# Last rows of the down weights by GpSimd's queue, and one value part ahead of their products, in a gated attention and feed-forward decode kernel

## The chip, the core and the metric

The kernel runs on one core of a Trainium2 chip. A core has TensorE (PE, with its weight loads shown apart as PEld), VectorE (DVE), ScalarE (ACT), GpSimd (POOL) and SyncE (SP), which run their own instruction streams and meet through semaphores, and 16 DMA engines that move data from device memory into the on-chip tiles of 128 partitions. The metric is the device time of one launch in microseconds (us). Before the change the median of 3 runs is 2518.33 us (2518.11 to 2518.47).

## The reference, cut to what is computed

One token decodes through a mix of two blocks: attention over a cache of 65,536 positions with 32 heads of 128, and a gated feed-forward block of width 1,792.

```python
def _A_ref(x, k_cache, v_cache, wq, wo):
    q = (x @ wq).reshape(B, Sq, H, Dh).transpose(0, 2, 1, 3)
    scores = jnp.einsum("bhqd,bhkd->bhqk", q, k_cache) * (Dh ** -0.5)
    p = _softmax(scores, axis=-1)
    o = jnp.einsum("bhqk,bhkd->bhqd", p, v_cache)
    return o.transpose(0, 2, 1, 3).reshape(B, Sq, H * Dh) @ wo

def _B_ref(x, w_gate, w_up, w_down):
    return (_silu(x @ w_gate) * (x @ w_up)) @ w_down

g = _sigmoid((x * gate_w).sum(-1, keepdims=True))
out = g * _A_ref(...) + (1 - g) * _B_ref(...)
```

All tensors are bfloat16. K and V have 537 MB each; all weights together are about 13.8 MB.

## The kernel before

K and V of a head come in two halves of 8.39 MB, each 256 cache rows per partition in 128 partitions. The big tile `ring` holds both halves of K (from byte 0 and 32 KB), both of V (96 KB and 112 KB), and, before the first and after the last use of those places, the weights: the query weights at first, then the output weights, gate and up weights, and the down weights (`WD`, from byte 64 KB, where the second half of K lay).

SP issues every large load, in one queue, in the order of its program: for each head the next K half, the V half, the other K half, the other V half, each as soon as PE or DVE has read what lay there (semaphores `ktd` for transposed K chunks, `va1` and `vbd` for read V halves). For each K chunk DVE transposes (L314) and PE takes the scores (L401). When a head's scores are complete, DVE takes the maximum, POOL reduces it over the partitions (L216), ACT takes the exponentials (L251) and POOL their sum (L218), and PE multiplies the values.

PE's program consists of named blocks joined by branches. `pe_ka` has a head's first 16 score chunks, `pe_vb` the second half of the previous head's values, `pe_kb` the last 16 score chunks and the first half of this head's values. The values of `pe_vb` come in the six parts of `PARTS`, with a semaphore each from `MARKS`: the first three (rows 192 to 256, 0 to 64, 64 to 128) by `flow`, 16 matmuls a part into `psW` (L417); then DVE copies `psW` to `brow` (L327, for the last head L355), PE adds its rows up (L452), and `values` does the other three parts with one matmul per row (L408). For the first 31 heads one load brings all six parts.

After the last head's scores the branch goes to `pe_mlp`. It does gate and up products (L488), waits for the activations `s_gu` and the down weights `s_wd`, multiplies the first 11 of the 14 down-weight columns (`WD_CUT`, `whole`, L428), lets ACT copy the row to `brow` (L266), puts that row into the two banks of the result (`rows`, L423 and L424), and jumps to `pe_vb` for the last head's second half. `pe_end` then adds the last three down-weight columns, each with its own semaphore (`s_wd1` to `s_wd3`), and the last head's part of the output product; DVE and ACT write the row out.

At the end of SP's list stand therefore: gate weights, up weights, the first 11 columns of the down weights, the last head's second value half in the six parts (the second to sixth after `va1`), and the last three columns of the down weights. All are issued by SP (L145).

Of the kernel before, what the change touches and what calls it, by code (L numbers as in the profile page):

```python
# [5 lines left out]
P = 128  # L6
# [4 lines left out]
V_A, V_B = 96 * KB, 112 * KB  # L11
# [15 lines left out]
def bass_gated_mix__mha_block_cached__swiglu_ffn__decode_kernel(  # L27
# [13 lines left out]
    _, H, S, Dh = A_k_cache.shape  # L41
    D = A_wq.shape[0]
    F = B_w_gate.shape[1]
    Dc = D // P
    FC = F // P
# [7 lines left out]
    PER = 2 * NCH  # L53

    with ExitStack() as ctx:
# [6 lines left out]
        def sem(name):  # L62
# [42 lines left out]
        hx = [kt[:, b, 0:FW].bitcast(F32) for b in range(3)]  # L105
        gu = kt[:, 3, 0:FW // 2].bitcast(BF16)
        guT = kt[:, 3, FW // 2:FW].bitcast(BF16)
        names = ("s_x s_wq s_k0a s_k0b s_ka s_kb s_va s_vb s_wo s_woc s_wg s_wu s_wd s_wd1 s_wd2 s_wd3 s_p2 s_p3 s_p4 s_p5 s_p6 "
                 "s_ones s_qd s_ramp s_rampT s_id s_sel s_z s_zb s_e1 s_g s_xT s_xTb s_q s_qTb s_qs s_zq s_h s_sig s_gu s_dch s_ach "
                 "ktd qkd va1 vbd s_mx s_ar s_nb s_exp s_pb s_L s_li s_otn s_o s_om s_y s_br s_fl s_flc s_id4 s_qr s_qc s_wod s_o31 s_y0 s_y1 s_fin s_out s_hot")  # L110
        sm = {n: sem(n) for n in names.split()}
# [7 lines left out]
        def at(byte, n):  # L119
            return ring[:, byte // 2:byte // 2 + n]  # L120

        WQ, WO, WG, WU, WD = 144 * KB, 0, 0, 14 * KB, 64 * KB
        PARTS = ((192, 256), (0, 64), (64, 128), (128, 168), (168, 184), (184, 192))
        FLOW = 3
        MARKS = ("s_vb", "s_p2", "s_p3", "s_p4", "s_p5", "s_p6")
        WD_CUT = FC - 3
        wq_ap = at(WQ, Dc * H * Dh).rearrange("p (c n) -> p c n", c=Dc)
        wg_ap = at(WG, Dc * F).rearrange("p (c m j) -> p c m j", c=Dc, j=FC)
        wu_ap = at(WU, Dc * F).rearrange("p (c m j) -> p c m j", c=Dc, j=FC)
# [12 lines left out]
        @block.sync  # L142
        def _(sp):
            def load(dst, src, s):
                sp.dma_start(dst, src).then_inc(sm[s], 16)  # L145

            def place(kind, h, u, s):
                byte = {"k": (K_A, K_B), "v": (V_A, V_B)}[kind][u]
                src = kv_dram[kind][:, u]
                if isinstance(h, int):  # L150
                    src = src[h]
                else:
                    src = src[bass.ds(h, 1)].rearrange("h p n -> (h p) n")
                load(at(byte, ROWS * Dh), src, s)

            k0 = kv_dram["k"][0, 0]
            k1 = kv_dram["k"][0, 1]
            half = ROWS * Dh // 2
            load(at(K_A + 2 * half, half), k0[:, half:2 * half], "s_ka")
            load(at(K_A, half), k0[:, 0:half], "s_k0a")  # L160
            load(at(K_B + 2 * half, half), k1[:, half:2 * half], "s_k0b")
            sp.wait_ge(sm["ktd"], NCH // 2)
            load(at(K_B, half), k1[:, 0:half], "s_kb")
            sp.wait_ge(sm["s_q"], 1)
            place("v", 0, 0, "s_va")

            def head(r, late):
                sp.wait_ge(sm["ktd"], r * PER + (PER - NCH // 2))
                place("k", r + 1, 0, "s_ka")
                sp.wait_ge(sm["va1"], r + 1)  # L170
                place("v", r, 1, "s_vb")
                if late:
                    wo_dram = A_wo.rearrange("(p j) n -> p (j n)", j=32)
                    for q in range(2):
                        sp.wait_ge(sm["ktd"], r * PER + (PER + 3 * NCH // 4 + q * NCH // 4))
                        load(at(WO + q * 16 * KB, 16 * D), wo_dram[:, q * 16 * D:(q + 1) * 16 * D], "s_wo")
                sp.wait_ge(sm["ktd"], r * PER + (PER + NCH // 2))
                place("k", r + 1, 1, "s_kb")
                sp.wait_ge(sm["vbd"], r + 2)
                place("v", r + 1, 0, "s_va")  # L180

            with nc.Fori(0, L - 1, engines=[ET.SP]) as i:
                head(i, False)
            head(L - 1, True)
            sp.wait_ge(sm["s_wod"], 1)
            load(at(WG, Dc * F), B_w_gate.rearrange("(p c) f -> p (c f)", c=Dc), "s_wg")
            load(at(WU, Dc * F), B_w_up.rearrange("(p c) f -> p (c f)", c=Dc), "s_wu")
            sp.wait_ge(sm["ktd"], PER * H)
            wd_dram = B_w_down.rearrange("(p c) n -> p (c n)", c=FC)
            load(at(WD, WD_CUT * D), wd_dram[:, 0:WD_CUT * D], "s_wd")  # L190
            last = kv_dram["v"][L, 1]
            for n, ((r0, r1), s) in enumerate(zip(PARTS, MARKS)):
                if n == 1:
                    sp.wait_ge(sm["va1"], H)
                load(at(V_B + r0 * 256, (r1 - r0) * Dh), last[:, r0 * Dh:r1 * Dh], s)
            for j, s in ((FC - 3, "s_wd1"), (FC - 2, "s_wd2"), (FC - 1, "s_wd3")):
                load(at(WD + 2 * j * D, D), wd_dram[:, j * D:(j + 1) * D], s)

        @block.gpsimd
        def _(pool):  # L200
            nc.gpsimd.memset(xTz[:], 0.0).then_inc(sm["s_qd"], 1)
            nc.gpsimd.memset(qd[:], 0.0).then_inc(sm["s_qd"], 1)
            for m, n in enumerate(MARKS[1:]):
                nc.gpsimd.memset(hbuf[:, m], 0.0).then_inc(sm[n], 16 * L)
            nc.gpsimd.memset(hot[:], 0.0).then_inc(sm["s_hot"], 1)
            pool.wait_ge(sm["s_id"], 1)
            pool.wait_ge(sm["s_hot"], 1)
            nc.gpsimd.tensor_copy(hot[:, 31:128:32], ident[:, P - 4:P])
            for je in range(4):
                off = 64 * (je // 2) + je % 2  # L210
                last = nc.gpsimd.tensor_copy(sel[:, je, :].rearrange("p (g d) -> p g d", g=4),
                                             ident[:, off:off + 63:2].unsqueeze(1).to_broadcast([P, 4, 32]))
            last.then_inc(sm["s_sel"], 1)
            for h in range(H):
                pool.wait_ge(sm["s_mx"], h + 1)
                nc.gpsimd.partition_all_reduce(amx, mxs, P, RMAX).then_inc(sm["s_ar"], 1)  # L216
                pool.wait_ge(sm["s_exp"], h + 2)
                nc.gpsimd.partition_all_reduce(Lt, rsum, P, RADD).then_inc(sm["s_L"], 1)  # L218

        @block.scalar  # L220
        def _(act):
# [140 lines left out]
        def _(pe):  # L362
# [14 lines left out]
            for b, bank in enumerate((psY, psZ)):  # L377
                for c in range(Dc):
                    for k in range(4):
                        n0 = (4 * b + k) * D  # L380
# [49 lines left out]
            only = [ET.PE]  # L430
# [14 lines left out]

            with nc.body("pe_vb", valid_engines=only):
                i = nc.snap(head, min_val=1, max_val=H)
                for n, ((r0, r1), s) in enumerate(zip(PARTS, MARKS)):
                    if n == FLOW:
                        pe.wait_ge(sm["s_flc"], i + 1)  # L450
                        for e in range(4):
                            nc.tensor.matmul(psO[:, 0:1], brow[:, e * Dh:(e + 1) * Dh], id4[:, e:e + 1],  # L452
                                             start=e == 0, stop=False)
                    pe.wait_ge(sm[s], i * 16)
                    if n < FLOW:
                        last = flow(V_B, 1, range(r0, r1), False, n == FLOW - 1)
                        if n == FLOW - 1:
                            last.then_inc(sm["s_fl"], 1)
                        continue
                    last = values(V_B, 1, range(r0, r1), False, n == len(PARTS) - 1)  # L460
                last.then_inc(sm["vbd"], 1)
                nc.br_lt(left, 2, on_true="pe_end", on_false="pe_next", engines=only)
# [17 lines left out]
            with nc.body("pe_mlp", valid_engines=only):  # L480
                pe.wait_ge(sm["s_wg"], 16)
                pe.wait_ge(sm["s_wu"], 16)
                pe.wait_ge(sm["s_woc"], 1)
                for w, bank in ((wg_ap, psY), (wu_ap, psZ)):
                    for c in range(Dc):
                        for g in range(4):
                            cols = w[:, c, 32 * g:32 * g + 32, :].rearrange("p m j -> p j m")
                            last = nc.tensor.matmul(bank[32 * g:32 * g + 32, 0:FW], xTz[:, 32 * c:32 * c + 32], cols,  # L488
                                                    start=(c == 0), stop=(c == Dc - 1))
                    last.then_inc(sm["s_h"], 1)  # L490
                pe.wait_ge(sm["s_gu"], 1)
                pe.wait_ge(sm["s_wd"], 16)
                for j in range(WD_CUT):
                    last = whole(guT[:, 32 * j:32 * j + 1], wd_ap[:, j, :], stop=(j == WD_CUT - 1))
                last.then_inc(sm["s_y"], 1)
                pe.wait_ge(sm["s_br"], 1)
                rows(onesr[0:1, 0:1], brow[0:1, :], first=True)
                nc.br("pe_vb", engines=only)

            with nc.body("pe_wo", valid_engines=only):  # L500
                pe.wait_ge(sm["s_otn"], H + 1)
# [62 lines left out]
```

## Time and profile before

| what | us |
|---|---|
| median of 3 runs | 2518.33 |
| the profiled execution, as timed | 2518.01 |
| its span, first to last instruction | 2516.6 |
| DVE busy | 1249.7 |
| PE busy | 1511.9 |
| POOL busy | 25.9 |

The difference of 1.4 us between the profiled execution and its span lies outside the first and last instruction. A line of a timeline gives start, duration, engine, source line, operation, output and inputs, and in brackets how long the engine was idle before and what released it. "DMA share" is the busy time of the transfers that begin in a stretch, as a share of 16 engines; in short stretches it can pass 1. SPq lines are DMA issues of SP. In the list of DMA issues the last number is the median time from issue to landing.

### The profile page before, as it was taken

How to read it: one execution, taken by the hardware profiler on the slowest of the kernel's cores; microseconds unless marked ns; L12 is line 12 of the kernel's file. 1: busy time of each engine (PE TensorE's matmuls, PEld its weight loads, DVE VectorE, ACT ScalarE, POOL GpSimd, SP SyncE). 2: the span in 40 equal slices, each digit the busy share in tenths (PEclk: the TensorE clock that was granted, in tenths of full speed). 3: DMA queues.
4: the chain of work that ended last, by engine and by line, in shares of the span. 5: the costliest groups of instructions: out<-in, count | busy, mean ns of one | idle time of the engine just before them, and what ended most of it. 6: DMA issues, size and time to landing. Idle time of an engine off the chain costs nothing.

```text
span 2516.6 us, 25250 instructions
## 1 busy us (share of the span) xinstructions
PE 1511.9 (60%) x10158; PEld 573.9 (23%) x10158; DVE 1249.7 (50%) x1213; ACT 43.0 (2%) x142; POOL 25.9 (1%) x81
## 2 busy tenths in 40 slices
PE   4565655745656556566565575565655655656568
PEld 1222222212222222222222121222212222212222
DVE  5454553644545536445455364464553644545534
ACT  0000000000000000000000000000000000000000
POOL 0000000000000000000000000000000000000000
PEclk8877877878778778778787787877877778778788
DMA  9999999999999999999999999999999999999999
GB/s 419 434 433 433 434 433 434 433 434 434 434 433 434 434 433 435 433 432 433 433 433 433 433 433 433 433 433 433 433 434 433 433 433 434 433 433 433 433 432 394
DMA packets 20748, 1087.73 MB, mean 432 GB/s; under 512 B 2307, under 2 KB 2694, under 8 KB 2950
## 3 DMA queue, kind: packets, MB, share of 16 engines
q1 hardware_dynamic: 20736, 1087.64, 99.9%
q8 instruction: 4, 0.07, 0.0%
q14 instruction: 2, 0.02, 0.0%
q10 hardware_dynamic: 6, 0.00, 0.0%
HBM read 1087.64 MB, written 0.00 MB: 432 GB/s over the span
## 4 chain that ended last, share of the span: by engine, by line
DMA 75%; DVE 15%; issue 7%; PE 2%; DVEq 1%; SPq 0%; ACT 0%; POOL 0%
DMA ring<-in_A_k_cache_dram 74%; DVE kt L314 15%; PE psS L401 2%; DMA ring<-in_A_v_cache_dram 1%; DVEq L311 0%; SPq L145 0%; PE psW L417 0%; DVE st L325 0%; PE psY L423 0%; ACT pa L251 0%; DVE pb L340 0%; DVE st L338 0%; DVEq L324 0%; DVE fin L359 0%; SPq L136 0%
## 5 line engine op out<-in xcount | busy, mean ns | idle before, releaser
L401 PE MATMUL psS<-kt,zq 128*128 128x512 bf16 x4096 | 1132.6, 425 | 854.6 <-DVE kt L314 835.3
L314 DVE STREAM_TRANSPOSE kt<-ring 128x1024 uint32<-128x1024 uint32 x1024 | 1163.1, 1206 | 939.7 <-DMA ring<-in_A_k_cache_dram 939.7
L401 PEld LDWEIGHTS psS<-kt,zq 128*128 128x128 bf16 x4096 | 385.1, 104 | 1588.3 <-DVE kt L314 1129.7
L417 PE MATMUL psW<-ring,pb 128*4 128x512 bf16 x3584 | 256.2, 448 | 102.7 <-DVE pb L340 102.4
L417 PEld LDWEIGHTS psW<-ring,pb 128*4 128x4 bf16 x3584 | 94.8, 98 | 262.6 <-issue 187.8
L327 DVE COPY brow<-psW 128x512 f32<-128x512 f32 x32 | 22.1, 691 | 120.5 <-PE psW L417 120.5
L408 PEld LDWEIGHTS psO<-pb,ring 128*128 128x128 bf16 x2048 | 57.0, 98 | 0.5 <-DMA ring<-in_A_v_cache_dram 0.2
L408 PE MATMUL psO<-pb,ring 128*128 128x1 bf16 x2048 | 56.6, 163 | 0.2
L330 DVE TENSOR_SCALAR lt<-psO,st,sc 128x4 f32 x32 | 9.4, 294 | 89.1 <-PE psO L408 89.1
L452 PE MATMUL psO<-id,brow 128*128 128x1 f32 x256 | 33.8, 253 | 25.5 <-DVE brow L327 24.7
L340 DVE STREAM_TRANSPOSE pb<-pa 128x512 bf16<-128x512 bf16 x32 | 22.8, 711 | 48.7 <-ACT pa L251 48.7
L249 ACT ACTIVATE st<-st 128x1 f32<-128x1 f32 x32 | 6.5, 203 | 2358.5 <-POOL st L216 2358.5
L338 DVE TENSOR_REDUCE st<-psS 128x1 f32<-128x512 f32 x32 | 22.1, 692 | 37.4 <-PE psS L401 37.4
L452 PEld LDWEIGHTS psO<-id,brow 128*128 128x128 f32 x256 | 31.0, 191 | 41.7 <-DVE brow L327 40.4
L216 POOL PARTITION_ALL_REDUCE st<-st x32 | 11.2, 351 | 2420.2 <-DVE st L338 2420.2
L251 ACT ACTIVATE pa<-psS,st 128x512 bf16<-128x512 f32 x32 | 22.0, 687 | 1.0
L428 PE MATMUL psF<-ring,om 128*1 (+1 forms) x32 | 12.7, 396 | 2.9 <-DMA ring<-in_A_wo_dram 2.9
L512 PE MATMUL psY<-ring,hot 128*128 (+1 forms) x32 | 13.1, 411 | 0.0
L218 POOL PARTITION_ALL_REDUCE st<-st x32 | 12.3, 383 | 36.4 <-ACT pa L251 36.4
L256 ACT COPY zq<-qd 128x16 bf16 x31 | 7.7, 248 | 0.0
L251 ACT ACTIVATION_READ_ACCUMULATOR pa<-psS,st 128x1 f32 x32 | 6.2, 193 | 0.0
L428 PE MATMUL psF<-ring,kt 128*1 128x512 bf16 x11 | 4.2, 564 | 3.0 <-DVE kt L353 3.0
(87 smaller groups left out, 52.8 us busy)
## 6 DMA issues: line engine op xcount, KB each, us to landing
ring<-in_A_k_cache_dram SPq DMA_DIRECT2D x4, 4096.0 KB, 27.4
ring<-in_A_v_cache_dram SPq DMA_DIRECT2D x3, 2048.0 KB, 17.6
ring<-in_A_wq_dram SPq DMA_DIRECT2D x1, 4096.0 KB, 12.4
ring<-in_A_wo_dram SPq DMA_DIRECT2D x2, 2048.0 KB, 10.6
ring<-in_B_w_gate_dram SPq DMA_DIRECT2D x1, 1792.0 KB, 21.4
ring<-in_B_w_up_dram SPq DMA_DIRECT2D x1, 1792.0 KB, 25.4
ring<-in_B_w_down_dram SPq DMA_DIRECT2D x1, 1408.0 KB, 13.1
ring<-in_A_v_cache_dram SPq DMA_DIRECT2D x1, 1280.0 KB, 20.4
```

Of the source, the lines that this page charges most:

```text
L218: nc.gpsimd.partition_all_reduce(Lt, rsum, P, RADD).then_inc(sm["s_L"], 1)
L251: nc.scalar.activation(pa[:], psS[:], ACT.Exp, bias=nbias, scale=SCALE, accum_out=rsum).then_inc(sm["s_exp"], 1)
L314: nc.vector.transpose(o, src).then_inc(sm["ktd"], 1)
L327: nc.vector.tensor_copy(brow[:], psW[:]).then_inc(sm["s_flc"], 1)
L338: nc.vector.reduce_max(mxs, psS[:], AX_X).then_inc(sm["s_mx"], 1)
L340: nc.vector.transpose(pb[:], pa[:]).then_inc(sm["s_pb"], 1)
L401: last = nc.tensor.matmul(psS[:], zw[je][c], ktb[n % NB][:, je // 2, :, je % 2], start=first and je == 0, stop=stop and je == 3)
L408: last = nc.tensor.matmul(psO[:, 0:1], at(base + r * 256, Dh), pb[:, col:col + 1], start=first and n == 0, stop=stop and n == len(rows) - 1)
L417: last = nc.tensor.matmul(psW[g:g + 4, :], pb[:, col:col + 97:32], at(base + r * 256, 4 * Dh), start=first and n < 4, stop=stop and n >= l ...
L428: return nc.tensor.matmul(psF[0:1, :], lhs, rhs, start=first, stop=stop)
L452: nc.tensor.matmul(psO[:, 0:1], brow[:, e * Dh:(e + 1) * Dh], id4[:, e:e + 1], start=e == 0, stop=False)
L512: return nc.tensor.matmul(psY[:], hot[:, bass.ds(31 - j, P)], w, start=first, stop=stop)
```

## The change

Three things are changed. SP's four loads of down weights cover the first 112 partitions (`WD_SP`) instead of 128. POOL, after its last reduction, waits for the last K chunk as SP does and issues the other 16 partitions' down weights: for each block of 8 partitions a DMA of 64 elements per partition and one of the remaining 7,104, all on a new semaphore `s_wp`. And `pe_vb` is split: its first part, rows 192 to 256, stays in `pe_vb`; the others are in a new block `pe_vb2`. The gate and up products of `pe_mlp` now branch to `pe_vb`, which for the last head branches to a new block `pe_down` with the down-weight products, and from there to `pe_vb2`; the products also wait for `s_wp`.

```diff
+        WD_SP = P - 16
...
-            load(at(WD, WD_CUT * D), wd_dram[:, 0:WD_CUT * D], "s_wd")
+            load(at(WD, WD_CUT * D)[0:WD_SP], wd_dram[0:WD_SP, 0:WD_CUT * D], "s_wd")
...
-                load(at(WD + 2 * j * D, D), wd_dram[:, j * D:(j + 1) * D], s)
+                load(at(WD + 2 * j * D, D)[0:WD_SP], wd_dram[0:WD_SP, j * D:(j + 1) * D], s)
...
                 nc.gpsimd.partition_all_reduce(Lt, rsum, P, RADD).then_inc(sm["s_L"], 1)
+            pool.wait_ge(sm["ktd"], PER * H)
+            wd_dram = B_w_down.rearrange("(p c) n -> p (c n)", c=FC)
+            for p0 in range(WD_SP, P, 8):
+                for n0, n1 in ((0, 64), (64, FC * D)):
+                    pool.dma_start(at(WD + 2 * n0, n1 - n0)[p0:p0 + 8],
+                                   wd_dram[p0:p0 + 8, n0:n1]).then_inc(sm["s_wp"], 16)
...
             with nc.body("pe_vb", valid_engines=only):
                 i = nc.snap(head, min_val=1, max_val=H)
-                for n, ((r0, r1), s) in enumerate(zip(PARTS, MARKS)):
+                pe.wait_ge(sm[MARKS[0]], i * 16)
+                flow(V_B, 1, range(*PARTS[0]), False, False)
+                nc.br_lt(left, 2, on_true="pe_down", on_false="pe_vb2", engines=only)
+
+            with nc.body("pe_vb2", valid_engines=only):
+                i = nc.snap(head, min_val=1, max_val=H)
+                for n, ((r0, r1), s) in list(enumerate(zip(PARTS, MARKS)))[1:]:
...
                     last.then_inc(sm["s_h"], 1)
+                nc.br("pe_vb", engines=only)
+
+            with nc.body("pe_down", valid_engines=only):
                 pe.wait_ge(sm["s_gu"], 1)
                 pe.wait_ge(sm["s_wd"], 16)
+                pe.wait_ge(sm["s_wp"], 64)
                 for j in range(WD_CUT):
                     last = whole(guT[:, 32 * j:32 * j + 1], wd_ap[:, j, :], stop=(j == WD_CUT - 1))
                 last.then_inc(sm["s_y"], 1)
                 pe.wait_ge(sm["s_br"], 1)
                 rows(onesr[0:1, 0:1], brow[0:1, :], first=True)
-                nc.br("pe_vb", engines=only)
+                nc.br("pe_vb2", engines=only)
```

More of the change, by code (lines that the diff above doesn't have):

```diff
@@ L107, in bass_gated_mix__mha_block_cached__swiglu_ffn__decode_kernel @@
         guT = kt[:, 3, FW // 2:FW].bitcast(BF16)
-        names = ("s_x s_wq s_k0a s_k0b s_ka s_kb s_va s_vb s_wo s_woc s_wg s_wu s_wd s_wd1 s_wd2 s_wd3 s_p2 s_p3 s_p4 s_p5 s_p6 "
+        names = ("s_x s_wq s_k0a s_k0b s_ka s_kb s_va s_vb s_wo s_woc s_wg s_wu s_wd s_wp s_wd1 s_wd2 s_wd3 s_p2 s_p3 s_p4 s_p5 s_p6 "
                  "s_ones s_qd s_ramp s_rampT s_id s_sel s_z s_zb s_e1 s_g s_xT s_xTb s_q s_qTb s_qs s_zq s_h s_sig s_gu s_dch s_ach "
```

## The prediction

> **What bounds the kernel now.** I read the head of the page first, then the DMA queues, then the chain that ended last, then the last microseconds in 0.2 us stretches.
>
> ```profile
> span 2516.6 us, 25250 instructions
> ...
> DMA packets 20748, 1087.73 MB, mean 432 GB/s; under 512 B 2307, under 2 KB 2694, under 8 KB 2950
> ## 3 DMA queue, kind: packets, MB, share of 16 engines
> q1 hardware_dynamic: 20736, 1087.64, 99.9%
> q8 instruction: 4, 0.07, 0.0%
> ```
>
> SP's queue (q1) keeps all 16 DMA engines at 99.9% of the span. Time is bytes, and the change moves none of them out of the program: 1087.64 MB stay. Nothing that shortens an engine's work in the 31 repeated heads can show; only the order in which the DMA engines finish can. The packets also tell how a transfer is cut: 144 transfers by SP's code, each of 128 rows and 16 small packets, are 144 x (128 + 16) = 20736. So a partition's row is one packet, and each engine carries 8 of the 128 rows.
>
> ```profile
> 2492.09 21.33 DMA ring<-in_A_v_cache_dram
> 2513.42 0.04 issue
> 2513.46 0.37 PE psO L408 x8
> ...
> 2514.98 0.41 DVE fin L359
> ```
>
> The chain's last long piece is V's last part. It lands at 2513.42; a fixed tail of 3.2 us follows to the span's end at 2516.6. Now the columns are stretch, length, busy times of PE, PEld, DVE, ACT and POOL, granted clock, DMA share and GB/s:
>
> ```profile
> 2495.00:2500.00 5.00, 2.87 (x16) 0.29 (x8) 4.57 (x4) 0.22 (x1) 0.00 (x0) 1.00 1.02 433
> ```
> ```profile
> 2512.00:2512.20 0.20, 0.20 (x13) 0.20 (x11) 0.00 (x0) 0.00 (x0) 0.00 (x0) 0.50 1.02 343
> 2512.20:2512.40 0.20, 0.20 (x14) 0.20 (x12) 0.00 (x0) 0.00 (x0) 0.00 (x0) 0.50 0.96 328
> 2512.40:2512.60 0.20, 0.20 (x13) 0.20 (x11) 0.00 (x0) 0.00 (x0) 0.00 (x0) 0.50 0.73 251
> 2512.60:2512.80 0.20, 0.17 (x7) 0.08 (x4) 0.00 (x0) 0.00 (x0) 0.00 (x0) 0.50 0.51 184
> 2512.80:2513.00 0.20, 0.19 (x7) 0.19 (x8) 0.00 (x0) 0.00 (x0) 0.00 (x0) 0.50 0.40 138
> 2513.00:2513.20 0.20, 0.20 (x13) 0.20 (x11) 0.00 (x0) 0.00 (x0) 0.00 (x0) 0.50 0.34 118
> 2513.20:2513.40 0.20, 0.20 (x8) 0.12 (x5) 0.00 (x0) 0.00 (x0) 0.00 (x0) 0.50 0.34 118
> 2513.40:2513.60 0.20, 0.14 (x6) 0.14 (x6) 0.00 (x0) 0.00 (x0) 0.00 (x0) 0.50 0.36 123
> 2513.60:2513.80 0.20, 0.20 (x10) 0.16 (x8) 0.00 (x0) 0.00 (x0) 0.00 (x0) 0.50 0.28 97
> 2513.80:2514.00 0.20, 0.20 (x4) 0.07 (x2) 0.13 (x1) 0.00 (x0) 0.00 (x0) 0.50 0.11 36
> ```
>
> The engines do not stop together. From 2513.0 to 2513.6 the share is 0.34, that is 0.34 x 16 = 5 engines still at work and 11 done. The ten shares sum to 5.05, times 0.2 us is 1.01 us: the mean engine stops at 2513.0, the last at about 2513.9. **Perfect balance could win 0.9 us, 0.04%**, and that is the ceiling for anything this change can gain.
>
> **The change, part by part.** *Rows taken from SP.* A row of down weights has 14,336 bytes (11,264 in the first transfer, three times 1,024). 433 GB/s at share 1.02 is 433/1.02/16 = 26.5 GB/s for one engine. 112 rows over 16 engines are 7 each instead of 8, so each engine is relieved of 14,336/26.5e3 = 0.54 us (0.43 us before V's parts). That is the end at -0.54 us, if the split stays even. The trace has no transfer of 112 rows; if its rows ran at half speed, 7 x 0.54 = 3.8 us would come on top, so the bounds are -0.54 and +3.2. I take -0.54: all transfers in the trace, of 16,384-byte and of 65,536-byte rows, run at one rate.
>
> *The same rows on GpSimd.* Four transfers of 8 rows. With whole rows as packets, one of them occupies at most 8 engines, so the two large ones put 2 x 14,208 bytes on the same 8 (with the two small, 28,672) or 14,208 on each of 16. The first gives 28,672/26.5e3 = 1.08 us on half the engines, net +0.54 there and -0.54 on the others; the second nets nothing. All 229,376 bytes on one engine would be 8.66 us, net +8.1. I take the same 8, because a small transfer of equal row count stands between the two large, so that an even rotation by 8 comes back to the same half. [...]
>
> A second queue on an engine has one price in the trace, the instruction packets:
>
> ```profile
> DMA packets 16, 1.00 MB, mean 500 GB/s; under 512 B 0, under 2 KB 0, under 8 KB 0
> ...
> q8 instruction: 1, 0.02, 3.2%
> ```
>
> In this 2.0 us stretch (2448 to 2450) one such packet takes 0.032 x 16 x 2.0 = 1.02 us; by the page's 0.07 MB in four it has 17.5 KB, 17 GB/s. At that rate the 28,672 bytes cost 1.69 us, net +1.15 on the loaded half. I keep 26.5 GB/s, since the destination is the tile that SP's rows go to, and +1.15 for the range.
>
> *Whether the loaded half holds a late engine* decides the sign. Five of 16 are late. Were their places independent, all five would be among the eight relieved in 56 of 4,368 choices, 1.3%; were they neighbours, about half the time. The trace does not name engines. I take one late engine loaded: **end +0.54 us**.
>
> *When GpSimd's rows are there, and the new wait.* POOL stands behind its last reduction:
>
> ```profile
> 2480.66 0.33 SPq L145 DMA_DIRECT2D ring<-in_B_w_down_dram  x1
> ...
> 2481.03 11.49 SPq L145 DMA_DIRECT2D ring<-in_A_v_cache_dram  x6
> ...
> 2484.07 0.38 POOL L218 PARTITION_ALL_REDUCE st<-st  x1 [1.14 <-ACT pa L251]
> ...
> 2492.56 1.38 SPq L145 DMA_DIRECT2D ring<-in_B_w_down_dram  x3
> ```
> ```profile
> 2500.12 0.65 DVE L353 STREAM_TRANSPOSE kt<-kt 128x448 bf16<-128x448 bf16 x1
> ...
> 2500.82 4.22 PE L428 MATMUL psF<-ring,kt 128*1 128x512 bf16 x11 [2.95 <-DVE kt L353]
> ...
> 2505.07 0.57 ACT L266 COPY brow<-psF 1x512 f32<-1x512 f32 x1 [9.86 <-PE psF L428]
> ...
> 2506.22 1.40 PEld L417 LDWEIGHTS psW<-ring,pb 128*4 128x4 bf16 x32 [0.44 <-issue]
> 2506.23 1.90 PE L417 MATMUL psW<-ring,pb 128*4 128x512 bf16 x32
> ...
> 2508.44 1.04 PE L417 MATMUL psW<-ring,pb 128*4 128x512 bf16 x16 [0.31 <-DMA ring<-in_A_v_cache_dram]
> 2509.53 0.69 DVE L355 COPY brow<-psW 128x512 f32<-128x512 f32 x1 [8.77 <-PE psW L417]
> 2510.28 1.04 PEld L452 LDWEIGHTS psO<-id,brow 128*128 128x128 f32 x8 [1.30 <-DVE brow L355]
> ...
> 2511.54 2.21 PEld L408 LDWEIGHTS psO<-pb,ring 128*128 128x128 bf16 x64 [0.22 <-DMA ring<-in_A_v_cache_dram]
> ```
> ```profile
> ring<-in_B_w_down_dram SPq DMA_DIRECT2D x1, 1408.0 KB, 13.1
> ring<-in_A_v_cache_dram SPq DMA_DIRECT2D x3, 2048.0 KB, 17.6
> ...
> ring<-in_A_k_cache_dram SPq DMA_DIRECT2D x62, 29.3
> ring<-in_B_w_down_dram SPq DMA_DIRECT2D x3, 128.0 KB, 21.1
> ```
>
> POOL is free at 2484.45, and nothing of POOL follows the DMAs. The trace has no issue by POOL; SP's three at 2492.56 take 1.38 us, 0.46 each, so I give four 1.8 us. Landing takes 13.1 to 21.1 us in SP's full queue, less in an empty one: 2499.4, or 2507.4 at worst. The products need the rows at 2500.82. Behind PE's wait stand the 11 products, ACT's copy L266, the two row sums and the rest of V. I cost it at nothing; the cover is 2500.82 - 2484.45 = 16.4 us. If it is gone, the path from the landing L is: products 4.2, copy and row sums 1.2, jump 0.4, two V parts 2.0, DVE copy and PE's sums 1.9, values about 1.8, the rest 2.3, so the end is L + 13.8 us; that passes 2516.6 only when L is later than 2502.8.
>
> *V's first part ahead of the products.* It lands at about 2481.03 + 17.6 = 2498.6, its 16 matmuls take 1.04 us, and a jump 0.44 (the idle time ahead of L417 at 2506.22): ready at 2500.1, before the products' input (DVE to 2500.77). After the products only one V part stands before the part that PE waits for at 2508.44, so the 0.31 us of idle time there grows by about 0.5. With unchanged landings that wins nothing; with landings 0.43 us earlier it lets PE follow.
>
> *The split block.* One more jump in each of 31 heads, at most 0.44 us, hidden behind the queue: a K load of 8.39 MB moves in 19.4 us at 433 GB/s but takes 29.3 us from issue to landing, so 9.9 us of transfers stand ahead of it. Cost nothing; with that cover gone 31 x 0.44 = 13.6 us.
>
> Sum: -0.54 + 1.08 = +0.54 on the late engine that ends the run. On this execution, 2518.01 us with 1.4 us around its span, that is 2518.55; it lies 0.32 below the median, so **2518.33 + 0.54 = 2518.9 us**.
>
> **The rivals.** *All late engines relieved.* The end comes 0.54 us earlier on them, and the early ones, done by 2513.0, move to 2513.5, so the gain stops near 0.45: 2517.9 us. For it speaks that the late ones are a group of five; against it, the 1.3%.
>
> *The halves take one large transfer each.* Every engine nets zero: 2518.3. Against it stands the small transfer between the two.
>
> *Slower: eight partitions limit the transfer, not the engine.* In every row of the trace 433 GB/s go to 128 partitions, 27 GB/s for eight. Were that a limit of the destination, each block of 8 x 14,336 bytes would hold its eight engines between 0.54 us (no limit) and 4.2 us, and the two blocks 1.08 to 8.5 us; net of the relief the loaded half ends +0.54 to +7.9 us later. I price it at the middle, +4.2: 2522.5 us. It decides as soon as a GpSimd row takes visibly longer than 0.54 us. For it: no row of the trace shows a transfer to few partitions. Against it: eight partitions at 27 GB/s and one engine at 26.5 GB/s are the same number in every row, so nothing says that the destination is the one that limits. [...]
>
> *GpSimd's rows are late, or lie on one engine.* L = 2507.4 gives an end of 2521.2, 4.6 us later: 2522.9 us; one engine gives 2526.4. Against the first stands an empty queue of its own.
>
> **How the numbers follow.** Forecast 0.47; all late ones relieved 0.18; one each 0.08; destination 0.19; late or one engine 0.08. A 0.2% step, 5.0 us, is about what a measurement of this kernel can tell from no change. The gains end at 0.9 us, so faster is 0.01. Slower takes the upper quarter of the destination case (0.05) and the one-engine part of the last (0.03): 0.08. The rest, 0.91, is no change that can be told. The range runs from 2517.6, under the relieved case, to 2521.5, which takes in the destination case up to about +3.2, and leaves out some 0.15. The forecast's own range is 2518.5 to 2519.6, up to the instruction packets' price.
>
> **What would show it.** A new queue with about 0.23 MB; POOL's four DMAs shortly after 2484.5; 16 matmuls on V ahead of the 11 products, which still wait for DVE's transpose and not for a DMA; PE waiting longer than 0.31 us for V's third part; shares in the last 2 us with a plateau that ends 0.54 us later if I am right, a short steep fall if the relieved case holds, and a low plateau of eight engines for several microseconds if the destination limits. A wait of the products on GpSimd's rows, a drop of SP's 99.9%, or a landing of the last weights more than 1 us later would prove me wrong.

## The result and the profile after

The changed kernel takes 2527.02 us (median of 7 runs, 2526.64 to 2527.49) against 2518.24 us before (7 runs): 8.8 us more, a ratio of 1.0035 with an interval of 1.0023 to 1.0047. The forecast was 2518.9 us in a range up to 2521.5, with 0.08 for a loss of more than 0.2%. The forecast loss was some 0.5 us, so it was wrong in size, and the result lies outside its range.

The head of the page after, and its DMA queues:

```profile
span 2525.8 us, 25319 instructions
...
DMA packets 20812, 1087.73 MB, mean 431 GB/s; under 512 B 2419, under 2 KB 2758, under 8 KB 3014
## 3 DMA queue, kind: packets, MB, share of 16 engines
q1 hardware_dynamic: 20672, 1087.42, 99.8%
q0 software_dynamic: 128, 0.23, 0.1%
```

The change did what it says: 0.23 MB moved from q1 to a queue of GpSimd's, and q1 lost 64 packets, 16 rows in each of four transfers. q1's busy share fell by 0.1 points only, and the new queue has those 0.1. The share can't show the loss: it adds up the time that packets took, and a slow packet takes more of it. The rate shows it. The stretches after, in the columns of the prediction's table (share and GB/s last):

```profile
2485.00:2490.00 5.00, 4.68 (x60) 1.76 (x64) 0.30 (x3) 0.00 (x0) 1.87 (x4) 0.66 1.08 381
2490.00:2495.00 5.00, 0.71 (x16) 0.15 (x8) 0.00 (x0) 0.00 (x0) 0.00 (x0) 1.00 0.99 151
2495.00:2500.00 5.00, 5.00 (x28) 0.84 (x24) 1.14 (x2) 0.54 (x1) 0.00 (x0) 0.66 1.01 161
2500.00:2505.00 5.00, 1.40 (x8) 0.00 (x0) 4.16 (x4) 0.00 (x0) 0.00 (x0) 1.00 0.97 367
...
2518.00:2520.00 2.00, 1.37 (x8) 1.36 (x8) 0.58 (x1) 0.00 (x0) 0.00 (x0) 0.78 1.00 325
2520.00:2522.00 2.00, 1.33 (x42) 1.18 (x42) 0.00 (x0) 0.00 (x0) 0.00 (x0) 0.50 0.51 154
2522.00:2524.00 2.00, 1.64 (x32) 1.09 (x32) 0.16 (x1) 0.00 (x0) 0.00 (x0) 0.50 0.06 18
```

and the same first four stretches of the kernel before:

```profile
2485.00:2490.00 5.00, 5.00 (x48) 1.62 (x52) 0.02 (x1) 0.00 (x0) 0.00 (x0) 0.50 0.97 412
2490.00:2495.00 5.00, 5.00 (x40) 1.17 (x36) 0.00 (x0) 0.33 (x1) 0.00 (x0) 0.94 1.04 440
2495.00:2500.00 5.00, 2.87 (x16) 0.29 (x8) 4.57 (x4) 0.22 (x1) 0.00 (x0) 1.00 1.02 433
2500.00:2505.00 5.00, 4.18 (x11) 1.19 (x11) 0.73 (x2) 0.00 (x0) 0.00 (x0) 0.66 0.99 423
```

For ten microseconds the engines are as busy as ever (shares 0.99 and 1.01) and deliver 151 and 161 GB/s instead of 440 and 433. Over the four stretches the rates differ by 31 + 289 + 272 + 56 = 648 GB/s, times 5 us is 3.24 MB, which at 433 GB/s is 7.5 us. The engines also stop less evenly: the shares 0.51 and 0.06 put the mean stop at 2521.1, and the last comes after 2523, 2 us behind, where it was 0.9 us before. Together that is 8.6 us, of the 9.3 us between the spans of the two profiled executions (2516.6 and 2525.8).

The timeline after shows who waited, with the idle time and its releaser in brackets:

```profile
2484.64 2.23 POOL L224 DMA_DIRECT2D ring<-in_B_w_down_dram  x4
...
2494.74 3.40 PE L501 MATMUL psY<-ring,xTz 128*32 128x448 bf16 x16 [4.29 <-issue]
...
2507.00 1.88 PE L424 MATMUL psW<-ring,pb 128*4 128x512 bf16 x16 [5.60 <-DMA ring<-in_A_v_cache_dram]
2508.66 4.34 PE L435 MATMUL psF<-ring,kt 128*1 128x512 bf16 x11
...
2516.79 1.04 PE L424 MATMUL psW<-ring,pb 128*4 128x512 bf16 x16 [1.56 <-DMA ring<-in_A_v_cache_dram]
```
```profile
ring<-in_B_w_down_dram POOLq DMA_DIRECT2D x2, 111.0 KB, 11.8
```

and the start of the gate and up products in the kernel before:

```profile
2491.20 3.43 PE L488 MATMUL psY<-ring,xTz 128*32 128x448 bf16 x16
```

GpSimd issues its four DMAs where expected, 0.56 us each. By the trace's packets its last row is there at 2498.0, and by its semaphore events the last increment of `s_wp` comes at 2500.4, well before PE's products begin (2508.66). PE waits for V: the part that it took up at 2508.44 is now there for 2516.79, 8.35 us later, after 1.56 us of idle time, and the end follows. Even the gate and up products start late (2494.74, before 2491.20): the up weights' semaphore, complete at 2490.3 before, now gets its last four increments between 2492.75 and 2494.64, and rows of up weights take up to 1.70 us instead of 0.54. The 15 of those rows that take 0.56 us or more begin between 2488.2 and 2490.4, when the first slow rows of down weights (from 2488.4) and GpSimd's first packets (from 2488.5) are under way.

### The profile page after: what moved, and what is told of

Read it like the earlier page. It is cut to its first block, busy times and chain, and to the rows that moved or that the text cites. A ratio compares the mean times of both kernels' runs of the same rounds, so it can differ in the third digit from the quotient of the medians.

```text
span 2525.8 us, 25319 instructions
## 1 busy us (share of the span) xinstructions
PE 1513.1 (60%) x10158; PEld 575.6 (23%) x10158; DVE 1249.8 (49%) x1213; ACT 43.0 (2%) x142; POOL 27.9 (1%) x85
## 4 chain that ended last, share of the span: by engine, by line
DMA 75%; DVE 15%; issue 7%; PE 2%; DVEq 1%; SPq 0%; ACT 0%; POOL 0%
DMA ring<-in_A_k_cache_dram 74%; DVE kt L321 15%; PE psS L408 1%; DMA ring<-in_A_v_cache_dram 1%; DVEq L318 0%; SPq L146 0%; PE psW L424 0%; DVE st L332 0%; PE psY L430 0%; ACT pa L258 0%; DVE pb L347 0%; DVE st L345 0%; DVEq L331 0%; DVE fin L366 0%; SPq L137 0%
```

## The experiments

Each is given against the kernel before on the same chip, with the ratio of the two times and its 95% interval in brackets. Where that interval takes in 1, the time alone does not tell the run from the kernel before, and the argument rests on the rate and on the time that single rows take.

**The two parts and the order, each alone.** The first keeps SP's 112 partitions and takes GpSimd's DMAs out:

```diff
-            pool.wait_ge(sm["ktd"], PER * H)
...
-                    pool.dma_start(at(WD + 2 * n0, n1 - n0)[p0:p0 + 8],
...
-                pe.wait_ge(sm["s_wp"], 64)
```

> SP's four loads of down weights cover 112 partitions; GpSimd's four DMAs and PE's wait for them are taken out, V's first part stays ahead of the products. Left out: the down weights of the last 16 partitions are not loaded, and the products use what stood in their place. [...] Theory B (GpSimd's blocks of 8 partitions hold up the engines): 0.5 us faster than before, the relief of 14,336 bytes per engine.

Measured: 2522.34 us, +4.1 us, ratio 1.0016 (1.0006 to 1.0025).

The second gives SP its 128 partitions back and lets GpSimd load its blocks into an unused place of the same partitions:

```diff
-        WD_SP = P - 16
+        WD_SP = P
...
-                    pool.dma_start(at(WD + 2 * n0, n1 - n0)[p0:p0 + 8],
+                    pool.dma_start(at(80 * KB + 2 * n0, n1 - n0)[p0:p0 + 8],
```

> SP's loads cover all 128 partitions again; GpSimd issues its four DMAs of 8 partitions as in the change, from the same weights, but into an unused place of the tile, and PE waits for them. 229 KB are loaded twice. [...] Theory B: 6 us or more slower. If both parts act (theory C), this and the 112-row run each lose some of the 8.8 us.

Measured: 2523.68 us, +5.4 us, ratio 1.0022 (1.0012 to 1.0031).

The third has the order alone: `WD_SP = P`, none of GpSimd's DMAs, no wait for them.

> Only the split of PE's block and V's first part ahead of the products; all down weights by SP in 128 partitions. [...] A loss here would mean that the extra jump in 31 heads or the new order costs time by itself.

Measured: 2518.48 us, +0.2 us, ratio 1.0001 (0.9992 to 1.0011): no difference that can be told.

The fourth, shown against the second, moves GpSimd's bytes in transfers of 128 partitions:

```diff
-            for p0 in range(P - 16, P, 8):
-                for n0, n1 in ((0, 64), (64, FC * D)):
...
+            for n0, n1 in ((0, 448), (448, 896)):
+                pool.dma_start(at(80 * KB + 2 * n0, n1 - n0), wd_dram[:, n0:n1]).then_inc(sm["s_wp"], 16)
```

> SP loads all 128 partitions; GpSimd issues two DMAs of 128 partitions by 448 elements, in all as many bytes as the change's four, into an unused place, and PE waits for them. Theory B in its form by destination (few partitions are slow): about 0.5 us slower than before, the price of 14,336 bytes on each of 16 engines. If a software queue beside SP's is slow by itself: 3 us or more slower. [...]

Measured: 2519.1 us, +0.85 us, ratio 1.0003 (0.9994 to 1.0013).

The stretch from 2490 to 2495 of these four, in this order:

```profile
2490.00:2495.00 5.00, 4.23 (x40) 1.04 (x36) 0.00 (x0) 0.00 (x0) 0.00 (x0) 0.90 1.03 242
```
```profile
2490.00:2495.00 5.00, 3.55 (x36) 0.90 (x32) 0.00 (x0) 0.00 (x0) 0.00 (x0) 0.88 1.04 198
```
```profile
2490.00:2495.00 5.00, 5.00 (x44) 1.12 (x40) 0.00 (x0) 0.12 (x1) 0.00 (x0) 0.93 1.02 433
```
```profile
2490.00:2495.00 5.00, 5.00 (x44) 1.13 (x36) 0.00 (x0) 0.05 (x1) 0.00 (x0) 0.90 1.04 438
```

Each of the change's two DMA edits brings the rate down by itself, to 242 and 198 GB/s at shares of 1.03 and 1.04; the order (433 GB/s), and a second queue with 128 partitions (438), do not. Theory C holds: 4.1 + 5.4 is 9.5, against 8.8 measured (the first leaves out 0.23 MB and the second loads them twice, so the bytes cancel). The fourth run also rules out that GpSimd's software queue is slow by itself, since it has the same queue and the same bytes at +0.85 us.

**Which partitions, at the same number of them.** SP loads 64 rows of the down weights, once 0 to 63 and once 32 to 95, all else as with the order alone:

```diff
-            load(at(WD, WD_CUT * D)[0:WD_SP], wd_dram[0:WD_SP, 0:WD_CUT * D], "s_wd")
+            load(at(WD, WD_CUT * D)[32:96], wd_dram[32:96, 0:WD_CUT * D], "s_wd")
...
-                load(at(WD + 2 * j * D, D)[0:WD_SP], wd_dram[0:WD_SP, j * D:(j + 1) * D], s)
+                load(at(WD + 2 * j * D, D)[32:96], wd_dram[32:96, j * D:(j + 1) * D], s)
```

> SP's four loads of down weights cover partitions 0 to 63 alone, 4 rows per engine; no DMA by GpSimd, V's first part ahead of the products. Left out: the down weights of partitions 64 to 127 are not loaded. [...] Theory E (only an engine's bytes count): rows at 0.42 us, V's parts 1.7 us earlier, about 1.2 us faster until PE's own chain holds. Theory U (any transfer of fewer than 128 partitions is slow): this one and the next are equally slow.

> The same number of rows and bytes, but partitions 32 to 95. Left out: the down weights of partitions 0 to 31 and 96 to 127. [...] Theory E: the same 1.2 us. Theory U: as slow as partitions 0 to 63.

Measured: partitions 0 to 63 take 2521.46 us, +3.3 us, ratio 1.0012 (1.0002 to 1.0022), with half of the down weights gone; partitions 32 to 95 take 2516.45 us, -1.75 us, ratio 0.9993 (0.9983 to 1.0002). Their stretches from 2488 to 2492, partitions 0 to 63 first:

```profile
2488.00:2492.00 4.00, 2.50 (x28) 0.78 (x20) 0.00 (x0) 0.00 (x0) 0.00 (x0) 0.76 1.13 231
```
```profile
2488.00:2492.00 4.00, 3.92 (x48) 1.12 (x40) 0.00 (x0) 0.00 (x0) 0.00 (x0) 0.90 1.01 426
```

231 against 426 GB/s: little more than half the rate for the same number of rows and bytes in other partitions. In the trace's packets a row of 11,264 bytes takes 0.87 us (median) with partitions 0 to 63 and 0.42 us with 32 to 95; before it was 0.43. So theory E, rows of 0.42 us in both runs, and theory U, two runs equally slow, do not hold. Against the order alone the run with partitions 0 to 63 ends 3.0 us later with half of the bytes gone: the slow rows also held up transfers of 128 rows before and after them, whose packets in this run go up to 1.75 us (up weights) and 1.59 us (V), where 0.55 and 0.62 were the longest before. And without slow rows the 32-to-95 run, of which no execution is as slow as any of the kernel before though its interval takes in 1, gained 2.0 us against the order alone. That is nearly all of the 2.16 us that four rows of 0.54 us make, an estimate with four rows fewer on each engine, not 1.2: PE's own chain did not hold it.

One rival is left. Row p of the down weights goes to partition p in every run, so the place in device memory that is read moves along with the partition that is written, and no run separates the two. For the partitions speaks that V's rows, which come from another tensor, slow down beside the slow rows (up to 1.59 us). It is shown that 64 rows are slow or not by which of them are loaded (0.87 and 0.42 us); the reason is not shown.

**The blocks without GpSimd, and with other partitions.** The blocks issued by SP, right behind its first load of down weights, which covers 128 partitions again; GpSimd issues nothing:

```diff
+            for p0 in range(P - 16, P, 8):
+                for n0, n1 in ((0, 64), (64, FC * D)):
+                    sp.dma_start(at(80 * KB + 2 * n0, n1 - n0)[p0:p0 + 8],
+                                   wd_dram[p0:p0 + 8, n0:n1]).then_inc(sm["s_wp"], 16)
             last = kv_dram["v"][L, 1]
```

> As the run with GpSimd's four DMAs alone (all 128 partitions by SP, blocks of 8 partitions into an unused place), but the blocks stand in SP's queue behind the first down weights. [...] Theory S (GpSimd's software queue beside SP's is what is slow): 0.5 to 1.1 us slower, the price of the bytes.

Measured: 2522.4 us, +4.2 us, ratio 1.0016 (1.0007 to 1.0026). The stretch from 2490 to 2495:

```profile
2490.00:2495.00 5.00, 5.00 (x44) 1.12 (x37) 0.00 (x0) 0.00 (x0) 0.00 (x0) 0.89 1.07 285
```

The same blocks are slow in SP's queue too (rows of 14,208 bytes at 0.60 to 1.42 us), and the end is at +4.2 us, so theory S does not hold.

GpSimd again, with 8 partitions four apart, shown against the run of GpSimd's blocks alone:

```diff
-            for p0 in range(P - 16, P, 8):
+            for p0 in (64, 65):
...
-                    pool.dma_start(at(80 * KB + 2 * n0, n1 - n0)[p0:p0 + 8],
-                                   wd_dram[p0:p0 + 8, n0:n1]).then_inc(sm["s_wp"], 16)
+                    pool.dma_start(at(80 * KB + 2 * n0, n1 - n0)[p0:p0 + 29:4],
+                                   wd_dram[p0:p0 + 29:4, n0:n1]).then_inc(sm["s_wp"], 16)
```

> As the run with GpSimd's four DMAs alone, with the same queue, sizes and number of partitions, but the 8 partitions of a DMA are 64, 68 and so on to 92, and 65 to 93, instead of 8 neighbours. [...] Theory S, or a limit that counts partitions: 5 us slower, as with the neighbours.

Measured: 2520.76 us, +2.6 us, ratio 1.0009 (1.0 to 1.0019), the rows of 14,208 bytes at 0.53 to 0.95 us. Half of the loss with neighbours (+5.4 us) is gone, but not all: the result lies between the price of the bytes, 1.08 us by the prediction's estimate, and the 5 us of a limit that counts partitions. The next run has `for p0 in (0, 1)` in its place:

> As GpSimd's DMAs to partitions 64, 68 and so on, with partitions 0, 4 and so on to 28, and 1 to 29. [...] If a row from GpSimd costs 2.5 us wherever it goes, it is 2.5 us slower again.

Measured: 2519.26 us, +1.05 us, ratio 1.0005 (0.9995 to 1.0014), all 16 rows at 0.53 to 0.54 us. The stretch from 2490 to 2495 with partitions 64 and up, then with 0 and up:

```profile
2490.00:2495.00 5.00, 3.25 (x24) 0.55 (x20) 0.00 (x0) 0.00 (x0) 0.00 (x0) 0.82 1.01 321
```
```profile
2490.00:2495.00 5.00, 4.60 (x32) 0.80 (x28) 0.00 (x0) 0.51 (x1) 0.00 (x0) 1.00 1.04 437
```

With partitions 0 to 29 the rate does not drop (437 GB/s, 440 before), and the end moves by about the price of 28,672 bytes, 1.08 us. So eight partitions are no limit by themselves. The last question was whether the order of the small and the large DMA counts:

```diff
-                for n0, n1 in ((0, 64), (64, FC * D)):
+                for n0, n1 in ((64, FC * D), (0, 64)):
```

> The same partitions 0, 4 and so on, but in each pair the large DMA is issued ahead of the small one. [...]

This run was made with `for p0 in (64, 65)`, not with the partitions that its expectation names. Measured: 2521.19 us, +3.0 us, ratio 1.0011 (1.0001 to 1.002), rows at 0.58 to 0.97 us: as slow as with the small DMA first.

> The last run, with the large DMAs first, was made with partitions 64, 68 and so on, not with 0, 4 and so on as its expectation says. So with partitions 64 both orders of large and small are known (+2.5 and +3.0 us), and with partitions 0 only the small first (+1.05). This is the missing one: partitions 0, 4 and so on to 28, and 1 to 29, the large DMAs first. [...] If GpSimd's 8 rows go to the same eight engines whatever stands ahead of them: rows at 0.53 us and 1.0 us slower, as with the small first.

Measured: 2519.7 us, +1.4 us, ratio 1.0005 (0.9995 to 1.0015), rows at 0.53 to 0.54 us. The stretch from 2490 to 2495 with the large DMAs first, partitions 64 and up, then 0 and up:

```profile
2490.00:2495.00 5.00, 3.18 (x28) 0.61 (x24) 0.00 (x0) 0.00 (x0) 0.00 (x0) 1.00 1.02 355
```
```profile
2490.00:2495.00 5.00, 4.43 (x32) 0.75 (x28) 0.00 (x0) 0.39 (x1) 0.00 (x0) 1.00 1.03 434
```

In both orders the rows take 0.53 to 0.54 us with partitions 0 to 29, and up to 0.95 and 0.97 us with 64 to 93, so a small DMA ahead makes no difference that these runs show. The trace names no engines: which ones carry the rows, and why partitions 0 to 29 cost less than 64 to 93, is not shown.

## Why the prediction was wrong, point by point

- *What bounds the kernel.* Right: PE's and DVE's own work was no part of the loss, and the last V parts' landing carried the end. "Time is bytes" was the flaw: the rate was 151 GB/s at a share of 0.99. Of the signs of being wrong, the last weights' landing came: 2523.6 by the semaphore events, 9.2 us later, where 1 us was the limit.
- *Rows taken from SP, -0.54 us.* This step failed. That each engine carries 7 rows instead of 8 was an estimate; the trace names no engines. That all transfers in the trace run at one rate was true of loads of 128 rows only, the only kind of load that SP's queue had. Alone, the 112 rows cost +4.1 us, above even the upper bound of +3.2; the bound priced the slow rows and not the V and up-weight rows that they hold up, which take up to 1.21 and 1.09 us in that run instead of 0.62 and 0.54. The median row of 11,264 bytes takes 0.76 us there. That the choice of partitions makes rows slow was shown for 64 rows; that the 112 are slow for the same reason is argued, since no run loads another 112.
- *GpSimd's rows at 26.5 GB/s, +1.08 us on half the engines.* This step failed for the partitions of the change, "since the destination is the tile that SP's rows go to": the partitions within the tile are what differs. It holds, as far as the interval can tell, with partitions 0 to 29 (+1.05 and +1.4 us). The blocks alone cost +5.4 us, and each of their rows took 0.61 to 2.0 us. The rival "eight partitions limit the transfer, not the engine" was therefore right that the destination counts, and wrong that a count of eight does: the eight partitions of the runs at 0 to 29 cost no more than their bytes. Its middle price, +4.2, is 4.8 before the relief is taken off, near the 5.4; it was given 0.19, and it was applied to GpSimd's blocks only, so its 2522.5 misses 2527.0 by the loss on SP's rows. The rival nearest in number, one engine for all of GpSimd's rows (2526.4), is near by luck: in the trace of the change several rows of each block are under way at once, the first eight within 3.2 us at 0.98 to 1.83 us each.
- *The same eight engines for both large DMAs.* Not shown, as the trace names no engines. With partitions 0 to 29 the end moves by +1.05 and +1.4 us, nearer to the estimate of 1.08 us for both on the same eight than to the 0.54 us for one on each half, with intervals that take in both. The even rotation over a small DMA in between was an assumption of mine that no run shows: their rows take 0.53 to 0.54 us behind the small DMAs and ahead of them.
- *A late engine in the loaded half.* It fits the +1.05 us of the run with partitions 0 to 29, if both large DMAs load the same eight engines there, 1.08 us by the prediction's estimate; a difference that small is within the interval. In the change itself it decided nothing.
- *Landing of GpSimd's rows, the wait, the order, the split block: nothing.* Right, the landing narrowly: the two large DMAs landed after a median of 11.8 us, against 13.1 to 21.1 in SP's queue before, and the last increment of `s_wp` came at 2500.4, under a cover that ended at 2500.82 before. PE's products never waited for the rows, and the order alone is within 0.2 us. In the change the products stand behind V's first part, for which PE waits until 2507.0, while their own input is ready at 2504.3; that cost nothing at the end, because PE still idles 1.56 us before V's third part.
- *The range.* It ended at 2521.5 by taking one upper bound of one case. Two transfers of a shape that the trace did not have were added, and their upper bounds belonged in one sum: 3.8 and 8.5 us less one relief of 0.54 are +11.7, and the measured 8.8 lies inside. The chances were also narrow by their own bounds: spread evenly, two fifths of the destination case lie above +5.0, not a quarter.

## What to carry to other kernels

A transfer that does not cover all 128 partitions has no price in a trace of transfers that all do: look at which partitions it loads (rows of 0.87 us with 0 to 63 and 0.42 with 32 to 95 here), not only at bytes per engine, and count two changed shapes as two risks that add. Where a queue is busy at 99.9%, read GB/s beside the share, since slow packets keep the share up (0.99 at 151 GB/s here). In these runs 8 rows in a transfer of their own cost more than their bytes, 1.08 us by estimate, with partitions 112 to 127 in either queue (+5.4 and +4.2 us) and with 64 to 93 (+2.6 and +3.0), and about their bytes with 0 to 29 only (+1.05 and +1.4); no run made the end earlier without leaving work out.

## What the runs showed of the hardware that I had not expected

Half the rows can cost more than all of them: 64 rows to partitions 0 to 63 end 3.3 us later than 128 rows, while 64 rows to partitions 32 to 95 end 1.75 us earlier (an interval that takes in no change). Slow rows spread: in the changed kernel rows of 16,384 bytes in V's parts, untouched by the change, take up to 2.65 us instead of 0.62, until 2502.5. And four DMA issues on GpSimd take 2.23 us of its time, 0.56 us each, with the first packet at 2488.5, 3.9 us after the first issue began.
